# A point of start, a bank and two planning times moved in a Nyström attention and MLP kernel

## The chip, the cores and the metric

The kernel runs on one core of one Trainium2 chip. The metric is device time in microseconds for one execution of the whole program: attention on 8 batches, a two-dimensional Fourier mix, a layer norm and an MLP. The engines are TensorE (PE in the profile, with PEld for its weight loads), VectorE (DVE), ScalarE (ACT), GpSimd (POOL) and SyncE (SP), whose queue issues the DMAs.

## The reference

```python
def _attn_ref(q, k, v):                      # (8, 8, 576, 64) each: batch, head, token, column
    q_lm = q.reshape(B, H, 32, S // 32, D).mean(axis=3)      # 32 landmarks, means of 18 tokens
    k_lm = k.reshape(B, H, 32, S // 32, D).mean(axis=3)
    A, Bm, C = sm(q, k_lm), sm(q_lm, k_lm), sm(q_lm, k)      # scaled softmax of a @ b.T
    Z = Bm.T / (norm(Bm, 1) * norm(Bm, inf) + 1e-06)
    for _ in range(6):
        Z = 2 * Z - Z @ Bm @ Z                               # Newton steps to the inverse
    return A @ Z @ C @ v

def _moe_ref(x, w_ch1, w_ch2):               # x: heads side by side, (8, 576, 512)
    u = x + real(fft(fft(x, axis=1), axis=2))
    un = (u - mean(u)) / sqrt(var(u) + 1e-06)
    return u + maximum(un @ w_ch1, 0.0) @ w_ch2              # 512 -> 2048 -> 512
```

The weights come as 64-bit floats, the rest as 32-bit floats.

## The kernel before

The program is written as a few Python generators ("threads") which take turns while the program is built: `attention` (and the threads it starts), `weights` and `mlp`. Each emits some instructions and then yields a waiting time. `self.now` is the planner's clock: each matmul moves it on by an assumed length, and a thread is taken up again when its time has come, the one of highest priority first. TensorE executes its instructions in just this order. On VectorE, ScalarE and GpSimd a scheduler sets the order; `Timed` (line 114) keeps a planned start for each of their instructions in a log. Where an instruction has a planned arrival `late` (or reads a tile that arrives by DMA), it must stand behind the last instruction of its engine whose planned start is not after `late`. So `late` keeps an instruction from standing ahead of what is planned sooner.

**Weights.** Each of the two matrices comes in NF = 16 pieces. A piece is loaded, decoded from 64-bit to 32-bit floats (`decoded` counts the pieces done, 32 in all), and then halved by `halve` into two fp16 tiles, hi by ScalarE and lo by VectorE (`w<-w,wsc` in the profile; `split_w` counts them). Before w2 can be halved, `scale` finds its scale: `wd`, `wm`, a matmul with ones, `wp_e`, a power on GpSimd (`wp_r`), `wsc`. Once all pieces are decoded, batch 1's q, k and v are loaded.

**MLP.** Tokens go through in chunks `ch` of 256. `h<-unT,w` are the first product's matmuls (24 for one h tile, into one of two h banks, `ps_h`); h is split in two fp16 parts (`u`, `unT`, `h` or `mid` as the room it lies in), and `acc<-w,...` are the second product's (12 for an h tile). The two accumulators of a chunk are read out by `u<-acc,wsc,u`, and only then may the next chunk's second product begin.

**Attention, one batch.** `tokens` sums the landmarks (`lm<-big`: one k sum and two q sums for each of two pairs of head groups, six in all), sums |q| on ScalarE (`amax`), and bounds k and q by powers of two: `kmax`, `qsum`, `aq_e`, `kb`, a matmul `kb,ones`, and `ak_e` (`bound`, line 261). With these it splits k's landmarks (`klm`, `kbd`) and q (`big<-big,aq_r`) into fp16 pairs, and goes on to the scores (`kbd,big`), their softmax (`amx`, `mid`, `asum`) and folds over tokens (`mid<-mid`). `landmarks` takes four of the four banks for attention, `ps_at`, for its matmuls (`at<-lm`, `at<-big,lm`), then makes the landmark softmax (`Bd`, `bs`, `nrm`, `BT`), C's exponentials (`mid<-at,cb`), and the Newton steps (`RE,E`). From batch 2 on, `values` turns C's exponentials over by DMA transposes (`th`) and adds their two parts (`mid<-mid 128x640`). `mix` multiplies everything together (`mid,big`, then `Wx`), with `w<-at,scw,w` and `u<-at,scw,w` on VectorE; `norm` normalises the new tokens (`bn`, `ve`, `r`, `row`). The first four tiles are transposed by TensorE, the later ones by DMA (`unT<-row`).

In batch 1 `tokens` begins when batch 0 is mixed far enough and `split_w[1]` has reached GATE = 8, half of w2. HOLD is an addition to two yields of batch 1 (ahead of the matmul on `kb`, ahead of the landmark matmuls). `there` is the planner's table of when a tile will be ready.

Of the kernel before, what the change touches and what calls it, by code (L numbers as in the profile page):

```python
# [10 lines left out]
F32 = mybir.dt.float32  # L11
# [7 lines left out]
P = 128  # L19
H, S, D, LM, DM, DF = 8, 576, 64, 32, 512, 2048  # L20
NF = DF // P
# [14 lines left out]
MARGIN, NM, AM, M0 = 1.5, 2.0, 2.0, 0.2  # L36

WT = 0.4

GATE = NF // 2  # L40

OFF = 768

PACE = 2

SPARE = 2

HOLD = 2.5

LATER = 5.0  # L50

# [107 lines left out]
class Kernel:  # L159
# [82 lines left out]
    def mm(self, out, a, b, start=True, stop=True, share=1.0):  # L242
        self.there[out.name] = self.now
        self.now += share * (1.0e-3 if a.dtype == F32 else 0.42e-3) * math.prod(b.shape[1:])
        self.nc.tensor.matmul(out, a, b, start=start, stop=stop, skip_group_check=True)  # L245

    def tr(self, out, a, ident):
        self.there[out.name] = self.now
        self.now += 0.11
        self.nc.tensor.transpose(out, a, ident)  # L250
# [7 lines left out]
        self.A.activation(hi, src, AF.Copy, scale=scale)  # L258
        self.V.scalar_tensor_tensor(lo, src, scale, hi, ALU.mult, ALU.subtract)

    def bound(self, cols, n, factor, name):

        ps = self.psum()
        self.mm(ps[:, :n], self.ones16, cols[:, :n])
        return self.power(ps[:, :n], n, factor, name)

# [155 lines left out]
    def tokens(self, b, st):  # L422

        nc, mm, mm3, tr, sm, split = self.nc, self.mm, self.mm3, self.tr, self.sm, self.split
        V, A = self.V, self.A
# [5 lines left out]
        qhs = []  # L431
        for e in range(2):
            kf, qf = loads[e][0][:, 0 : 2 * S], loads[e][1][:, 0:NQ]
            first = V.tensor_reduce(lm[:, 1, e], kf.rearrange("p (m t) -> p m t", t=18), AX.X, ALU.add)
            if b == 1:
                self.tc.keep_in_program_order(first)

            lv = lm[:, 0, e].rearrange("p (x o m) -> p x o m", o=2, m=8)
            qv = qf.rearrange("p (x o t) -> p x o t", o=2, t=2 * SEG)
            for o in range(2):  # L440
                first = V.tensor_reduce(lv[:, :, o], qv[:, :, o, o : o + 144].rearrange("p x (m t) -> p x m t", t=18), AX.X, ALU.add)
                if b == 1:
                    self.tc.keep_in_program_order(first)
            qhs.append(self.big().bitcast(F16))
            A.activation((self.whole[0].bitcast(F16) if b == 0 else qhs[e])[:, 0:NQ], qf, AF.Abs, accum_out=am[:, e : e + 1])
            yield self.till(lm)
        kb = self.small(2, "kb", BF16)
# [5 lines left out]
        V.tensor_tensor(qs, am[:, 0:1], am[:, 1:2], ALU.add)  # L453
        eq, rq = self.power(qs, 1, 2.0**-13, "aq", b == 1)
        V.tensor_tensor(kb[:, 0:1], km, eq, ALU.mult)
        yield self.till(kb, banks=1, more=AM) + (HOLD if b == 1 else 0.0)
        ek, rk = self.bound(kb, 1, 2.0**-13, "ak")
        sc = self.small(2, "sc")
        V.tensor_tensor(sc[:, 0:1], eq, rk, ALU.mult)
        V.tensor_scalar(sc[:, 1:2], ek, 1.0 / 144.0, None, ALU.mult)  # L460
# [19 lines left out]
        for u in range(3):  # L480
            yield self.till(*qhs, banks=1)
            ps = self.psum()
# [27 lines left out]
        for u in range(3):  # L510
            ae, w = aes[u], 512 if u < 2 else 128
            AT = (self.mid() if u < 2 else self.row()).bitcast(F16)[:, 0 : 2 * w].rearrange("p (y t) -> p y t", y=2)
            if b < 2:
                yield self.till(ae, banks=1)
                ps = self.psum()
# [3 lines left out]
            if b >= 2 or u == 2:  # L519
                yield self.till(ae)  # L520
                hl = self.row(2 * w, F16).rearrange("p (y t) -> p y t", y=2)
# [43 lines left out]
    def values(self, b, st, loads, Ces, crs, ci):  # L565

        nc, mm, tr, sm = self.nc, self.mm, self.tr, self.sm
        V, A = self.V, self.A
        R0 = sm.tile([P, 2, 64], F32, name="R0", bufs=1)
        ETs = []  # L570
        for g in range(2):
            yield self.till(Ces[g])
            if b < 2:
                ET = self.mid().rearrange("p (t m) -> p t m", t=5)
                ps = self.psum()
                for t in range(4):
                    tr(ps[:, 128 * t : 128 * t + 128], Ces[g][:, 128 * t : 128 * t + 128], self.ident)
                A.copy(ET[:, 0:4].rearrange("p t m -> p (t m)"), ps)
                ps = self.psum()
                tr(ps[:64, 0:128], Ces[g][:, 512:576], self.ident)  # L580
                A.copy(ET[:64, 4], ps[:64, 0:128])
            else:

                hl, th = (self.mid().bitcast(F16).rearrange("p (y t) -> p y t", y=2) for _ in range(2))
                A.copy(hl[:, 0], Ces[g])
                self.G.tensor_tensor(hl[:, 1], Ces[g], hl[:, 0], ALU.subtract)
                for y in range(2):
                    nc.sync.dma_start_transpose(th[:, y].rearrange("p (t m) -> p t m", m=P), hl[:, y])
                self.there[th.name] = self.there[hl.name] + 4.0
                self.slow.add(th.name)  # L590
                V.tensor_tensor(Ces[g], th[:, 0], th[:, 1], ALU.add)
                ET = Ces[g].rearrange("p (t m) -> p t m", t=5)
            ETs.append(ET)
        for g in range(2):
            yield self.till(ETs[g], loads[0][2], loads[1][2], banks=1)
            vfs = [loads[e][2].rearrange("p (c d) -> p c d", c=5) for e in range(2)]
            ps = self.psum()
            for t in range(5):
                n = P if t < 4 else 64
                for i in range(4):  # L600
                    e, at = divmod(sum(GROUPS, []).index(HEADS[g][i]), 4)
                    v = vfs[e][:n, t, 64 * at : 64 * at + 64]
                    mm(ps[32 * i : 32 * i + 32, 0:64], ETs[g][:n, t, 32 * i : 32 * i + 32], v if at % 2 == i % 2 else v[:, ::-1], t == 0, t == 4)
            V.tensor_scalar(R0[:, g], ps[:, 0:64], crs[g], ci[:, g : g + 1], ALU.mult, ALU.mult)
        st["R0"] = R0

    def landmarks(self, b, st):
# [11 lines left out]
        while b == 1 and self.seconds < NF // 2 - HB:  # L619
            yield 0.5  # L620
        yield self.till(lm, banks=4) + (HOLD if b == 1 else 0.0)
        heads = [(slice(64 * g, 64 * g + 64), slice(32 * r, 32 * r + 32), g, r // 2, r % 2) for r in range(4) for g in range(2)]
# [358 lines left out]

    def attention(self):
        for b in range(self.NB):
            while self.folded < b - 1 or (b > 0 and self.split_w[1] < GATE):
                yield 0.5
            yield from self.tokens(b, {"AT": []})

# [98 lines left out]
```

## Time and profile before

| what | value |
|---|---|
| median of 3 runs | 1006.84 us (1006.77 to 1008.21) |
| the profiled execution | 1008.58 us, of it 1006.8 in the span |
| mean granted TensorE clock | 0.976 |
| TensorE busy | 959.8 us (95%) |
| VectorE, ScalarE, GpSimd busy | 600.5, 333.0, 102.8 us |
| instructions | 20849 |

All times of the trace are microseconds from the first instruction. A profile line gives engine, source line, operation, `out<-in` by tile names, the shape, and a count. Nearly all instructions carry the line of a helper (L138, L245, L250), so they are told apart by their tiles. Lines of waits name the engine, what waited, what it waited for, then the total, the number of times, and the longest.

### The profile page before, as it was taken

The page shows a single profiled execution, that of the slowest core. Times are in us where ns is not written, and L with a number is a line of the kernel's source. Part 1 is how long each engine was busy: PE and PEld are TensorE (multiplying, and loading weights), DVE is VectorE, ACT ScalarE, POOL GpSimd, SP SyncE. Part 2 cuts the span into 40 slices and gives each one's busy share as a digit, 9 for nine tenths or more (in the row PEclk, how much of TensorE's full clock was granted, in tenths as well). Part 3 has the DMA queues.
Part 4 walks back from the last instruction along what each step waited for, and adds up shares of the span by engine and source line. Part 5 has one row for each costly group of instructions (what it writes and reads, how often), then busy time and mean ns, then how long its engine had stood idle before and what let it go on. Part 6 is the DMA issues. An engine that isn't in the chain of part 4 may idle for free.

```text
span 1006.8 us, 20849 instructions
## 1 busy us (share of the span) xinstructions
PE 959.8 (95%) x8698; PEld 666.9 (66%) x8698; DVE 600.5 (60%) x1629; ACT 333.0 (33%) x716; POOL 102.8 (10%) x114
## 2 busy tenths in 40 slices
PE   6869989699999999999999999999999999999998
PEld 4658556467766767667666677676666776666665
DVE  7989876878476836388367736684643935241111
ACT  5668543243224322143224222332322323111110
POOL 0000000003011301032012201120020210010000
PEclk8879989989999999999999999999999999999999
DMA  9854104123302340134211340225020200120000
GB/s 330 290 210 145 62 2 169 22 54 83 136 17 48 63 157 12 32 51 100 100 43 29 45 168 9 55 44 187 1 53 22 53 10 22 22 54 21 1 21 21
DMA packets 97774, 74.66 MB, mean 74 GB/s; under 512 B 68112, under 2 KB 86544, under 8 KB 97552
## 3 DMA queue, kind: packets, MB, share of 16 engines
q1 hardware_dynamic: 97680, 73.34, 25.4%
q8 instruction: 68, 1.11, 0.4%
q14 instruction: 26, 0.21, 0.1%
HBM read 48.02 MB, written 9.44 MB: 57 GB/s over the span
## 4 chain that ended last, share of the span: by engine, by line
PE 86%; DVE 9%; ACT 2%; DMA 2%; issue 1%; POOL 1%; SPq 0%; DVEq 0%; ACTq 0%; POOLq 0%
PE acc L245 36%; PE h L245 36%; PE at L245 13%; DVE w L138 2%; DVE mid L138 1%; DVE u L138 1%; DVE lm L138 1%; DMA big<-k_dram 1%; PE at L250 1%; DVE row L138 0%; ACT w L138 0%; DMA mid<-mid 0%; DMA out_dram<-u 0%; DVE asum L138 0%; DVE bn L138 0%
## 5 line engine op out<-in xcount | busy, mean ns | idle before, releaser
L245 PE MATMUL h<-unT,w 128*128 128x256 f16 x3456 | 411.4, 273 | 6.7 <-DMA unT<-row 5.4
L245 PEld LDWEIGHTS <-w 128*128 128x128 f16 (+1 forms) x3584 | 346.0, 99 | 80.9 <-DMA unT<-row 5.8
L245 PE MATMUL acc<-w,h 128*128 128x512 f16 x1632 | 386.2, 382 | 1.8 <-DVE w L138 1.8
L245 PEld LDWEIGHTS <-h 128*128 128x128 f16 x1632 | 157.8, 99 | 166.6 <-issue 14.2
L138 DVE SCALAR_TENSOR_TENSOR h<-h 128x512 f16<-128x512 f32 x136 | 93.6, 688 | 207.1 <-ACT h L138 206.7
L138 ACT ACTIVATE h<-h 128x512 f16<-128x512 f32 x136 | 81.0, 596 | 319.2 <-PE h L245 313.1
L138 POOL TENSOR_TENSOR r<-ve,mhalf 128x2 f32<-128x2 f32 (+1 forms) x20 | 13.8, 689 | 495.7 <-DVE ve L138 477.0
L138 DVE TENSOR_REDUCE lm<-big 128x32 f32<-128x576 f32 (+1 forms) x48 | 44.4, 938 | 3.3 <-DMA big<-k_dram 3.1
L245 PEld LDWEIGHTS <-big 128*128 128x128 f16 (+1 forms) x864 | 40.5, 104 | 8.5 <-issue 2.1
L138 DVE TENSOR_TENSOR mid<-mid 128x256 f32<-128x256 f32 (+3 forms) x64 | 38.4, 633 | 7.9 <-DMA mid<-mid 6.4
L138 POOL TENSOR_TENSOR mid<-mid 128x640 f16<-128x640 f32 (+1 forms) x24 | 30.6, 1292 | 117.0 <-ACT mid L138 102.5
L245 PEld LDWEIGHTS <-mid 64*128 64x128 f16 (+1 forms) x624 | 29.2, 95 | 17.1 <-issue 10.8
L138 POOL TENSOR_TENSOR row<-row 128x512 f16<-128x512 f32 (+1 forms) x33 | 34.1, 1048 | 50.1 <-ACT row L138 50.1
L138 DVE SCALAR_TENSOR_TENSOR u<-at,scw,w 128x128 f32<-128x128 f32 (+3 forms) x105 | 33.7, 388 | 7.2 <-PE at L245 5.5
L138 ACT CAST row<-row 128x512 f16<-128x512 f32 (+1 forms) x40 | 20.8, 551 | 51.6 <-DVE row L138 44.6
L138 DVE SCALAR_TENSOR_TENSOR w<-at,scw,w 128x262 f32<-128x262 f32 (+1 forms) x42 | 19.1, 486 | 29.7 <-ACT w L138 29.6
L138 DVE SCALAR_TENSOR_TENSOR u<-acc,wsc,u 128x512 f32<-128x512 f32 x36 | 26.9, 749 | 11.8 <-PE acc L245 11.7
L245 PE MATMUL at<-mid,big 128*128 128x262 f16 (+1 forms) x288 | 33.2, 289 | 0.0
L245 PEld LDWEIGHTS at<-RE,E 128*128 128x128 f32 x192 | 26.8, 194 | 8.4 <-issue 2.8
L245 PE MATMUL at<-RE,E 128*128 128x64 f32 (+1 forms) x192 | 28.8, 273 | 3.2 <-DVE E L138 2.5
L138 DVE SCALAR_TENSOR_TENSOR big<-big,aq_r 128x1024 f16<-128x1024 f32 (+1 forms) x32 | 25.8, 840 | 3.5 <-ACT big L138 3.5
L138 DVE TENSOR_TENSOR E<-at,mask 128x256 f32<-128x256 f32 x40 | 16.7, 418 | 18.3 <-PE at L245 18.3
(178 smaller groups left out, 916.8 us busy)
## 6 DMA issues: line engine op xcount, KB each, us to landing
w<-w_dram SPq DMA_DIRECT2D x22, 512.0 KB, 7.0
big<-v_dram SPq DMA_DIRECT2D x16, 640.0 KB, 9.5
big<-q_dram SPq DMA_DIRECT2D x16, 584.0 KB, 6.1
big<-k_dram SPq DMA_DIRECT2D x16, 576.0 KB, 5.2
out_dram<-u SPq DMA_DIRECT2D x36, 256.0 KB, 2.0
big<-w_dram SPq DMA_DIRECT2D x10, 512.0 KB, 6.6
t<-t_dram SPq DMA_DIRECT2D x1, 1048.0 KB, 10.6
unT<-row SPq DMA_TRANSPOSE x64, 2.4
```

The lines of the kernel that those rows point to most:

```text
L138: ins = call(out, *args, **kw)
L245: self.nc.tensor.matmul(out, a, b, start=start, stop=stop, skip_group_check=True)
L250: self.nc.tensor.transpose(out, a, ident)
```

## The change

Batch 1's tokens begin once all 32 pieces are decoded, in place of once half of w2 is halved. HOLD becomes 0. Batch 1's matmul on `kb` writes into an h bank instead of an attention bank. The landmark sums (and `amax` with the first) get `late = now`. The planned arrival of the DMA-transposed C tiles is 6.5 behind the split in place of 4.0.

```diff
-GATE = NF // 2
-HOLD = 2.5
+HOLD = 0.0
-    def bound(self, cols, n, factor, name):
-        ps = self.psum()
+    def bound(self, cols, n, factor, name, apart=False):
+        ps = self.ps_h.tile([P, 512], F32, name="h") if apart else self.psum()
...
             kf, qf = loads[e][0][:, 0 : 2 * S], loads[e][1][:, 0:NQ]
+            V.late = A.late = self.now
             first = V.tensor_reduce(lm[:, 1, e], ...)
...
             for o in range(2):
+                V.late = self.now
                 first = V.tensor_reduce(lv[:, :, o], ...)
...
-        yield self.till(kb, banks=1, more=AM) + (HOLD if b == 1 else 0.0)
-        ek, rk = self.bound(kb, 1, 2.0**-13, "ak")
+        yield self.till(kb, banks=b != 1, more=AM) + (HOLD if b == 1 else 0.0)
+        ek, rk = self.bound(kb, 1, 2.0**-13, "ak", b == 1)
...
-                self.there[th.name] = self.there[hl.name] + 4.0
+                self.there[th.name] = self.there[hl.name] + 6.5
...
-            while self.folded < b - 1 or (b > 0 and self.split_w[1] < GATE):
+            while self.folded < b - 1 or (b > 0 and self.decoded < 2 * NF):
                 yield 0.5
```

No instruction is added or removed; the orders change from w2's scale on. Three places, in the order in which the engines execute (`w_73` is the tensor of w1, `w_74` that of w2; the source lines move by two).

First, VectorE from w2's scale to the landmark sums of batch 1. Before:

```order
L138 TENSOR_SCALAR wp_e<-at 128x1
L138 TENSOR_SCALAR wp_r<-wp_r 128x1
L138 RECIPROCAL wp_e<-wp_r 128x1
L138 TENSOR_SCALAR wsc<-wp_r 128x1
L138 SCALAR_TENSOR_TENSOR u<-h,u 128x512
L138 TENSOR_SCALAR wsc<-wp_e 128x1
L138 SCALAR_TENSOR_TENSOR w_74<-w_74,wsc 128x512 x3
L138 SCALAR_TENSOR_TENSOR unT<-h,unT 128x512
L138 SCALAR_TENSOR_TENSOR w_74<-w_74,wsc 128x512 x5
L138 TENSOR_REDUCE lm<-big 128x64
L138 TENSOR_REDUCE lm<-big 128x4x8 x2
```

After:

```order
L136 TENSOR_REDUCE lm<-big 128x64
L136 TENSOR_REDUCE lm<-big 128x4x8 x2
L136 TENSOR_SCALAR wp_e<-at 128x1
L136 SCALAR_TENSOR_TENSOR u<-h,u 128x512
L136 TENSOR_SCALAR wp_r<-wp_r 128x1
L136 RECIPROCAL wp_e<-wp_r 128x1
L136 TENSOR_SCALAR wsc<-wp_r 128x1
L136 TENSOR_SCALAR wsc<-wp_e 128x1
L136 SCALAR_TENSOR_TENSOR w_74<-w_74,wsc 128x512 x2
L136 SCALAR_TENSOR_TENSOR unT<-h,unT 128x512
L136 SCALAR_TENSOR_TENSOR w_74<-w_74,wsc 128x512
L136 TENSOR_REDUCE lm<-big 128x64
```

The first three sums have moved from behind eight splits of w2 to ahead of its scale, the next three from behind the ninth split to behind the third. On TensorE, the matmul on `kb` stood behind the landmark matmuls, in an attention bank:

```order
L245 MATMUL acc_1680<-w_74,h 128x512
L245 MATMUL at<-lm 32x32 x8
L245 MATMUL at<-big,lm 32x288 x16
L245 LDWEIGHTS ones_102
L245 MATMUL at<-kb,ones_102 128x1
```

and now stands after 18 of the 24 matmuls of an h tile, 27 second-product matmuls ahead of the landmark matmuls:

```order
L243 LDWEIGHTS w_73
L243 MATMUL h<-unT,w_73 128x256
L243 LDWEIGHTS ones_102
L243 MATMUL h<-kb,ones_102 128x1
L243 LDWEIGHTS w_73
```

The bank it writes is one of the two for h.

Second, VectorE where the first chunk's accumulators are read out, in batch 1's softmax. Before:

```order
L138 SCALAR_TENSOR_TENSOR unT<-h,unT 128x512
L138 TENSOR_REDUCE asum<-mid 128x16
L138 TENSOR_TENSOR row<-at,amx 128x128
L138 TENSOR_SCALAR asum<-asum 128x16
L138 SCALAR_TENSOR_TENSOR u<-acc_1680,wsc,u 128x512
L138 RECIPROCAL asum<-asum 128x16
L138 TENSOR_REDUCE asum<-row 128x4
L138 SCALAR_TENSOR_TENSOR u<-acc_1681,wsc,u 128x512
```

After:

```order
L136 SCALAR_TENSOR_TENSOR row<-at,row 128x128
L136 TENSOR_TENSOR row<-row 128x128
L136 TENSOR_TENSOR mid<-mid 128x512
L136 TENSOR_TENSOR mid<-mid 128x256 x2
L136 TENSOR_TENSOR E<-at,mask 128x256
L136 TENSOR_TENSOR mid<-mid 128x256 x2
L136 TENSOR_TENSOR mid<-mid 128x512
L136 TENSOR_TENSOR RE<-RE,at 128x2x32
L136 TENSOR_TENSOR mid<-mid 128x512
L136 SCALAR_TENSOR_TENSOR u<-acc_1683,wsc,u 128x512
L136 SCALAR_TENSOR_TENSOR u<-acc_1684,wsc,u 128x512
```

The two readings now stand behind the folds of batch 1.

Third, VectorE in batch 1's `mix` and `norm`, where batch 2's sums stood. Before:

```order
L138 BN_AGGR mv<-bn 128x2
L138 TENSOR_REDUCE lm<-big 128x4x8
L138 BN_AGGR mv<-bn 128x2
L138 SCALAR_TENSOR_TENSOR h<-h 128x512
L138 TENSOR_SCALAR ve<-mv 128x2
L138 TENSOR_REDUCE lm<-big 128x4x8
L138 TENSOR_TENSOR rt<-r_2574 128x2
L138 TENSOR_REDUCE lm<-big 128x64
L138 SCALAR_TENSOR_TENSOR rt<-rt,ve 128x2
L138 TENSOR_REDUCE kmax<-lm 128x1
L138 SCALAR_TENSOR_TENSOR r_2576<-rt,r_2574 128x2
L138 SCALAR_TENSOR_TENSOR w_74<-at,scw,w_73 128x262
```

After:

```order
L136 BN_AGGR mv<-bn 128x2 x2
L136 TENSOR_SCALAR ve<-mv 128x2
L136 TENSOR_TENSOR rt<-r_2531 128x2
L136 SCALAR_TENSOR_TENSOR rt<-rt,ve 128x2
L136 SCALAR_TENSOR_TENSOR r_2533<-rt,r_2531 128x2
L136 TENSOR_SCALAR row<-u,mv,r_2533 128x512 x2
L136 SCALAR_TENSOR_TENSOR h<-h 128x512
L136 TENSOR_TENSOR row<-row 128x512 x2
L136 SCALAR_TENSOR_TENSOR w_74<-at,scw,w_73 128x262 x2
```

Batch 2's sums have gone behind the second `norm` of batch 1; here `w_73` and `w_74` name rooms at the end of the weights' tensors that `mix` uses. On SP the loads, the stores and the transposes of unT keep their order; in three later batches the last transposes of the softmax tiles are issued in another order among themselves. On GpSimd nothing moves.

## The prediction

> **What bounds the kernel now.** I began with busy time by engine, on the page (share of the span, instructions).
>
> ```profile
> PE 959.8 (95%) x8698; PEld 666.9 (66%) x8698; DVE 600.5 (60%) x1629; ACT 333.0 (33%) x716; POOL 102.8 (10%) x114
> ```
>
> TensorE is busy for 959.8 of 1006.8 us; nothing else comes near. The change removes no matmul and adds none, so it can move the time in two ways only: through the 47 us in which TensorE stands idle, and through the granted clock. The next view is busy time by stretch (PE, PEld, DVE, ACT, POOL, then clock, DMA share, GB/s).
>
> ```profile
> 120.00:140.00 20.00, 14.17 (x98) 5.81 (x97) 17.96 (x58) 10.81 (x24) 0.00 (x0) 0.83 0.00 0
> 200.00:220.00 20.00, 18.82 (x157) 12.40 (x165) 13.51 (x35) 7.74 (x13) 1.42 (x4) 0.82 0.27 55
> 400.00:450.00 50.00, 50.00 (x424) 33.88 (x423) 26.24 (x80) 14.68 (x31) 7.63 (x10) 1.00 0.22 39
> ```
>
> From 120 to 140 TensorE is idle for 5.8 us and its clock at 0.83; from 200 to 220 the clock is 0.82. In the last row TensorE is full, 50.00 of 50.00, as in nearly all later stretches. Up to 109 us the order of the work stays as it is. So the change is decided between 109 and 220 us, in batch 1. Who held TensorE there (waits of PE, 120 to 270 us: total, times, longest):
>
> ```profile
> PE h L245 <- DMA unT<-row: 5.4, 2, 3.2
> PE at L245 <- ACT mid L138: 4.0, 1, 4.0
> PE at L245 <- DVE w L138: 2.4, 1, 2.4
> PE acc L245 <- DVE w L138: 1.8, 1, 1.8
> PE acc L245 <- DVE u L138: 1.4, 1, 1.4
> ```
>
> That is 15.0 us. Two of these waits are followed by slow matmuls; TensorE's timeline (start, length, count, wait ahead):
>
> ```profile
> 112.43 10.90 PE L245 MATMUL acc<-w,mid 128*128 128x512 f16 x48
> 126.04 2.54 PE L245 MATMUL acc<-w,h 128*128 128x512 f16 x11 [1.84 <-DVE w L138]
> 133.75 0.16 PE L245 MATMUL at<-kb,ones 128*128 128x1 bf16 x1 [3.99 <-ACT mid L138]
> 133.78 6.48 PE L245 MATMUL acc<-w,h 128*128 128x512 f16 x18
> 185.31 2.79 PE L245 MATMUL h<-unT,w 128*128 128x256 f16 x24
> 201.18 3.81 PE L245 MATMUL h<-unT,w 128*128 128x256 f16 x17 [2.19 <-DMA unT<-row]
> 204.92 1.52 PE L245 MATMUL at<-mid,big 128*64 128x262 f16 x12
> 307.64 0.86 PE L245 MATMUL at<-mid,big 128*64 128x262 f16 x12
> ```
>
> The fourth row against the second: 18 at the second's pace (11 in 2.54, so 0.215 apart and the last some 0.38 long) are 4.04 us, so 2.4 are lost to the clock. The sixth against the fifth (0.109 apart): 17 are 2.0, 1.8 lost; the seventh against the eighth: 0.7 lost. Waits and clock together are 15.0 + 2.4 + 2.5 = 19.9 us, and the first row is 0.4 over 48 at full pace: 20.3 us could at most be won here.
>
> **Part 1, an earlier start and a bank apart: the wait of 3.99 goes.** The matmul on kb waited for one of four attention banks, all held by the landmark matmuls until ScalarE had read the first. In the h bank, and placed ahead of the landmark matmuls, it waits for kb alone. It costs 0.03 us of TensorE (133.75 to 133.78). No row shows an h bank held for it; the bounds are 0 and one VectorE split of an h tile, 0.68 in the row of 111.13 below. I take 0, because the bank's next h tile comes 24 h matmuls and more later. Gain: 3.99 + 2.4.
>
> **Part 2, what the sums now stand ahead of.** The first three landmark sums stand ahead of the last steps of w2's scale (wp_e), the next three ahead of w2's fourth split, not its ninth and tenth.
>
> ```profile
> 108.89 0.29 DVE L138 TENSOR_REDUCE wm<-wd 128x1 f32<-128x128 f32 x1
> 109.99 0.16 DVE L138 TENSOR_SCALAR wp_e<-at 128x1 f32<-128x1 f32 x1 [0.82 <-PE at L245]
> 110.81 0.15 DVE L138 TENSOR_SCALAR wp_r<-wp_r 128x1 int32<-128x1 int32 x1 [0.66 <-POOL wp_r L138]
> 111.13 0.68 DVE L138 SCALAR_TENSOR_TENSOR u<-h,u 128x512 f16<-128x512 f32 x1
> 112.00 2.47 DVE L138 SCALAR_TENSOR_TENSOR w<-w,wsc 128x512 f16<-128x512 f32 x3
> 119.42 2.67 DVE L138 TENSOR_REDUCE lm<-big 128x64 f32<-128x1152 f32 x3
> 109.87 0.60 ACT L138 ACTIVATE u<-h 128x512 f16<-128x512 f32 x1 [2.53 <-PE h L245]
> 111.25 1.33 ACT L138 ACTIVATE w<-w,wsc 128x512 f16<-128x512 f32 x2 [0.78 <-DVE wsc L138]
> ```
>
> The sums run from 109.1 to 111.8 (2.67); wp_e follows, wp_r 0.82 after it (109.99 to 110.81), the u split inside that gap, and ScalarE's first half of a piece 0.44 after wp_r: 113.0 in place of 111.25. TensorE is there at 112.43, has the first half at 113.7 and VectorE's at 114.5, and loses 0.2 on the next piece: 1.3 + 0.6 + 0.2 = 2.1 us waited. The splits go at 0.86 apart (2.47 for three): two, the unT split, a third to 116.6, three sums to 119.2, the fourth to 119.9. TensorE wants the fourth at 117.95: 1.95. The old wait of 1.84 on the tenth piece and the 0.4 are gone. The sum over |q| (ScalarE) moves into the idle 2.53 ahead of 109.87 and costs nothing; without that cover it would delay the u split by less than those 2.53. No DMA moves here: batch 1's loads are issued at the same place as before, and POOL's order is unchanged.
>
> Then TensorE has 8 matmuls left of the piece (1.7), 24 h (2.6), 27 acc (5.8), the landmark matmuls (1.2) and 18 acc (3.9): it asks for nrm at 135.2. VectorE meanwhile has five splits to 124.4, q's scaling, klm, kbd and five splits more, to 133.1, and only then Bd.
>
> ```profile
> 130.53 0.28 DVE L138 TENSOR_SCALAR Bd<-at 128x32 f32<-128x32 f32 x2
> 133.08 1.26 DVE L138 SCALAR_TENSOR_TENSOR big<-big,aq_r 128x1024 f16<-128x1024 f32 x1
> 134.87 0.18 DVE L138 TENSOR_TENSOR nrm<-diag,rs 128x64 f32<-128x64 f32 x1
> ```
>
> From Bd to nrm were 4.5 us, 1.26 of it q's scaling, which has left; two splits have come in (1.4): nrm at 133.1 + 4.6 = 137.7, a new wait of 2.5. At this point the same matmul work is done as before at 140.1: ahead by 2.4.
>
> **Part 3, the softmax of batch 1.** The score matmuls are now cut into the Newton steps; a bank free only after VectorE's subtraction holds a transpose for 1.0, and one Newton step waits 0.7 behind a split. Then the first accumulator has to be read out (u<-acc) before ch 1's second product may begin. That was placed amid the softmax; now it stands behind all folds.
>
> ```profile
> 153.10 0.75 DVE L138 SCALAR_TENSOR_TENSOR u<-acc,wsc,u 128x512 f32<-128x512 f32 x1
> 153.90 0.81 PE L245 MATMUL acc<-w,u 128*128 128x512 f16 x3 [1.38 <-DVE u L138]
> 158.54 0.28 DVE L138 SCALAR_TENSOR_TENSOR row<-at,row 128x128 f16<-128x128 f32 x1
> 161.98 0.69 DVE L138 TENSOR_TENSOR mid<-mid 128x512 f16<-128x512 f32 x1
> ```
>
> Row split to last fold are 4.1 us (158.54 to 162.67). By the same steps from 137.7 the row split comes at 152.2, so u<-acc runs 156.3 to 157.0; TensorE is ready at 154.0. New wait 3.0 in place of 1.38.
>
> **Part 4, sums behind batch 1's norm.** Four sums of batch 2 stood in the chain from `w` to the transposes.
>
> ```profile
> 184.66 1.34 DVE L138 TENSOR_REDUCE lm<-big 128x64 f32<-128x1152 f32 x1
> 189.01 0.72 DVE L138 TENSOR_REDUCE lm<-big 128x32 f32<-128x576 f32 x1
> 191.42 1.34 DVE L138 TENSOR_REDUCE lm<-big 128x64 f32<-128x1152 f32 x1
> 193.47 0.99 DVE L138 TENSOR_SCALAR row<-u,mv,r 128x512 f32<-128x512 f32 x2
> 194.69 23.71 SPq L907 DMA_TRANSPOSE unT<-row  x10
> ```
>
> Without 1.34 + 0.72 + 1.34 the rows come some 3.3 us sooner against the first mixing matmuls, the transposes too (6.5 us from the first issue to the matmul at 201.18). TensorE now also has 27 acc and 48 h between those matmuls and ch 2's first, 11.0 us at the paces above and some 2 of mixing (12 acc and 24 h before). From the end of the first mixing (185.31) to 201.18 were 15.9 us; less 3.3 that is 12.6, against 13 of work: no wait is left of the 5.4, nor the clock's 2.5. The second `w` now stands behind the row splits, so of the 2.4 wait 0.9 stays.
>
> **Part 5, the rest.** 6.5 for 4.0 in `there` lengthens no transfer, it moves the adds of the transposed tiles in the plan. The one place where such an add held TensorE:
>
> ```profile
> 559.57 0.82 DVE L138 TENSOR_TENSOR mid<-mid 128x640 f32<-128x640 f16 x1 [2.23 <-DMA mid<-mid]
> 560.87 0.63 PE L245 MATMUL at<-RE,E 128*128 128x64 f32 x4 [2.46 <-DVE E L138]
> 561.93 4.45 PE L245 MATMUL acc<-w,h 128*128 128x512 f16 x12
> ```
>
> There the second add stands ahead of E in the new order too: I take 0. It is worth 2.46 + 1.7 (4.45 against 2.75 for 12 at full pace) either way: if it vanished a gain, if batch 2, where one add now stands ahead of ci, repeated it a loss. Batch 2's nrm comes 1.0 late by the same walk (its sums begin later). In batches 3 to 7 TensorE's work ahead covers the later sums (the full row of 400 us); bounds plus or minus 1 us, taken as 0.
>
> **The clock.** 2.46 us idle were enough for the slow matmuls just shown; after 1.84 the row at 126.04 ran at full pace. The new waits are 2.1, 1.95, 2.5 and 3.0; I count one slow stretch, 2.5 us, like the other two. [...]
>
> **Sum.** Gone: 3.99 + 2.4 + 1.84 + 0.4 + 1.38 + 2.4 + 5.4 + 2.5 = 20.3. New: 2.1 + 1.95 + 2.5 + 1.7 + 3.0 + 0.9 + 1.0 + 2.5 = 15.7. Net -4.6: a span of 1002.2 for 1006.8. The profiled run took 1008.58, 1.8 over its span; the median of the runs, 1006.84, stands at the span itself, so I forecast 1002.2.
>
> **Rivals.**
> - The clock stays full: the new waits are spread and each is under 3.2. The same sum without 2.5: 999.7. For it: 1.84 left the clock at full; against it: 2.46 did not, and 2.5 and 3.0 are expected. [...] 0.22.
> - The waits only change place: every wait of 2 us and over brings a slow stretch (three, not one): 1002.2 + 5 = 1007.2, no change; with two 1004.7. 0.18.
> - Slower: ch 2's first matmuls still wait for the transposes. For it: the walk leaves them 0.4 us of slack, and they are one queue (ten within 23.71 us). If something holds them there, the 5.4 and 2.5 stay: 1002.2 + 7.9 = 1010.1. Against it: nothing new stands ahead of them on SP. It decides from some 5 us later than walked (0.4 of slack, 4.2 of wait and the clock's 2.5 take back 6.7, to 1008.9). 0.10.
> - The new waits are mostly hidden, as my walk errs towards waiting (it adds every semaphore step): 995. 0.08.
>
> **How the numbers follow.** The forecast has 0.42, its own range 999.9 to 1004.5. From 996.5 to 1007.5 lie the forecast, the full clock and the changed places, 0.82; 995 and 1010 lie outside. A difference under 0.2% (2 us) is about what a measurement can't tell from none. Faster by more, below 1004.8: 0.41 + 0.22 + 0.08 = 0.71; within, 1004.8 to 1008.9: 0.19; slower: 0.10.
>
> **What would show it.** In the new trace: no wait ahead of kb; PE waits on `w` near 112 and 118 us, on nrm near 135, on `u` near 154; ch 2's first h matmuls without a wait on unT; clock under 1.00 in at most one stretch between 120 and 220. Wrong would be: a wait of over 3 us on unT, or new waits beyond 260 us.

## The result, and the profile after

The changed kernel took 1021.43 us (median of 4 runs, 1020.36 to 1022.83) against 1007.40 for the kernel before: 1.014 times as long (95% interval 1.0122 to 1.0157). The forecast was 1002.2, in a range to 1007.5: it is slower, not faster. The profiled execution took 1020.54, of it 1018.5 in the span. Busy time by engine:

```profile
PE 963.1 (95%) x8698; PEld 667.6 (66%) x8698; DVE 600.4 (59%) x1629; ACT 331.2 (33%) x716; POOL 99.7 (10%) x114
```

TensorE is busy 3.3 us longer for the same matmuls but for the bank of one (963.1 against 959.8). The granted clock does not explain that, for its mean was 0.979 here and 0.976 before; it stays open. The other 8.4 us of the longer span are idle time. Busy time by stretch (TensorE's stands first, its clock third from the end), the three rows shown of before and one more:

```profile
120.00:140.00 20.00, 17.99 (x166) 10.38 (x165) 18.91 (x66) 13.71 (x29) 0.00 (x0) 1.00 0.01 1
200.00:220.00 20.00, 18.17 (x165) 11.72 (x163) 17.53 (x59) 9.12 (x21) 3.06 (x5) 1.00 0.23 58
400.00:450.00 50.00, 50.00 (x419) 33.24 (x417) 25.15 (x59) 13.24 (x23) 6.89 (x9) 1.00 0.22 38
310.00:330.00 20.00, 17.44 (x134) 9.85 (x133) 15.82 (x53) 8.70 (x20) 1.78 (x2) 0.83 0.11 34
```

Batch 1 is better than before: from 120 to 140 us TensorE stands idle for 2.0 in place of 5.8 us, and the clock is full. The row at 400 us, on which the prediction leant for batches 3 to 7, is as full as it was. But from 310 to 330 us there are 2.6 us of idle time and a clock of 0.83. TensorE's timeline in batch 1:

```profile
113.17 0.38 PE L243 MATMUL acc<-w,mid 128*128 128x512 f16 x1 [1.10 <-ACT w L136]
119.33 1.02 PE L243 MATMUL acc<-w,mid 128*128 128x512 f16 x4 [1.75 <-DVE w L136]
136.89 0.46 PE L243 MATMUL at<-nrm,ones_bd 128*128 128x128 f32 x2 [2.01 <-DVE nrm L136]
156.02 5.73 PE L243 MATMUL acc<-w,u 128*128 128x512 f16 x18 [2.70 <-DVE u L136]
201.62 2.78 PE L243 MATMUL h<-unT,w 128*128 128x256 f16 x24
```

These are the waits that the prediction named, at the places it named; ch 2's h matmuls run without a wait on unT. TensorE's waits beyond 200 us, of the changed kernel (the first four rows) and, beyond 210 us, of the kernel before (the last two):

```profile
PE at L243 <- ACT mid L136: 6.2, 4, 2.4
PE at L243 <- DVE E L136: 5.5, 2, 3.0
PE at L243 <- DVE u L136: 5.1, 2, 2.6
PE at L243 <- DVE nrm L136: 0.5, 1, 0.5
...
PE at L245 <- DVE E L138: 2.5, 1, 2.5
PE at L245 <- DVE u L138: 1.6, 2, 0.8
```

17.3 us against 4.1: the loss lies beyond batch 1. Three chains carry it. The first, in batch 2 (timelines of VectorE, ScalarE and TensorE):

```profile
209.99 0.28 DVE L136 TENSOR_REDUCE kmax<-lm 128x1 f32<-128x128 f32 x1
211.01 2.81 ACT L136 ACTIVATE big<-big,aq_r 128x1024 f16<-128x1024 f32 x4 [3.66 <-DVE kb L136]
213.72 0.24 ACT L136 ACTIVATE Bd<-Bd 128x64 f32<-128x64 f32 x1
213.99 0.22 DVE L136 TENSOR_REDUCE bs<-Bd 128x2 f32<-128x64 f32 x1 [1.47 <-ACT Bd L136]
215.45 0.16 PE L243 MATMUL at<-kb,ones 128*128 128x1 bf16 x1 [1.29 <-ACT mid L136]
```

The sums, `kmax` and q's bound come so late that ScalarE, idle for 3.66 us, splits q just when Bd's exponential is due. VectorE waits for it with `bs`, and `cb` behind; so the exponentials that would free an attention bank come late, and TensorE waits for that bank with `kb`. The second, also in batch 2, and the third, in batch 3:

```profile
225.68 0.82 DVE L136 TENSOR_TENSOR mid<-mid 128x640 f32<-128x640 f16 x1 [2.21 <-DMA mid<-mid]
228.04 0.71 PE L243 MATMUL at<-RE,E 128*128 128x64 f32 x4 [3.00 <-DVE E L136]
...
319.98 0.28 DVE L136 TENSOR_SCALAR Bd<-at 128x32 f32<-128x32 f32 x2
320.55 0.98 DVE L136 SCALAR_TENSOR_TENSOR u<-at,scw,w 64x256 f32<-64x256 f32 x3
321.07 1.72 PE L243 MATMUL at<-big,lm 64*32 64x288 f32 x16 [2.56 <-DVE u L136]
322.72 4.02 PE L243 MATMUL h<-unT,w 128*128 128x256 f16 x18
```

An add waits 2.21 us for its DMA ahead of E; and the last `u` of a mix, which frees the bank of the landmark matmuls, now stands behind Bd, and with it behind two of q's splits (1.54 us from 318.53). The 18 h matmuls after that wait take 4.02 us (2.13 at 206.83 in the same trace, where the clock is 1.00): from 320.6 to 327.4 us the granted clock is 0.50.

### The profile page after: what moved, and what is told of

It is laid out like the page before. It is cut to its first block, busy times and chain, and to the rows that moved or that the text cites. A ratio compares the mean times of both kernels' runs of the same rounds, so it can differ in the third digit from the quotient of the medians.

```text
span 1018.5 us, 20860 instructions
## 1 busy us (share of the span) xinstructions
PE 963.1 (95%) x8698; PEld 667.6 (66%) x8698; DVE 600.4 (59%) x1629; ACT 331.2 (33%) x716; POOL 99.7 (10%) x114
## 4 chain that ended last, share of the span: by engine, by line
PE 64%; DVE 8%; issue 4%; ACT 2%; DMA 1%; POOL 1%; SPq 1%; POOLq 0%; DVEq 0%; ACTq 0%
PE h L243 28%; PE acc L243 27%; PE at L243 10%; DVE lm L136 1%; DVE big L136 1%; DVE u L136 1%; DVE h L136 1%; DMA mid<-mid 1%; ACT big L136 1%; DVE mid L136 1%; POOL row L136 1%; DVE row L136 1%; SPq L588 0%; DVE cmx L136 0%; ACT h L136 0%
## 5 line engine op out<-in xcount | busy, mean ns | idle before, releaser
L243 PE MATMUL acc<-w,h 128*128 128x512 f16 x1632 | 382.2, 380 | 0.0
```

## The experiments

In the table each ratio is to the kernel before on the same chip.

| run | us | ratio, 95% interval |
|---|---|---|
| n1_no_late | 1006.54 | 0.9982 (0.9967 to 0.9998) |
| n2_late_alone | 1022.91 | 1.0142 (1.0113 to 1.0171) |
| n3_four_back | 1023.93 | 1.0157 (1.0127 to 1.0187) |
| n4_start_alone | 1004.45 | 0.9959 (0.9945 to 0.9973) |
| n5_bank_for_all | 1026.63 | 1.0186 (1.0165 to 1.0206) |
| n6_late_but_3_and_7 | 1016.32 | 1.0081 (1.0060 to 1.0102) |
| n7_start_and_bank | 1005.77 | 0.9979 (0.9968 to 0.9990) |
| n8_start_adds_behind | 1000.87 | 0.9933 (0.9917 to 0.9950) |
| n9_changed_adds_behind | 1013.36 | 1.0052 (1.0034 to 1.0070) |
| n10_best_plus_bank | 1002.56 | 0.9935 (0.9911 to 0.9960) |
| n11_best_hold_0 | 1000.86 | 0.9917 (0.9892 to 0.9942) |
| n12_best_late_in_2 | 997.78 | 0.9896 (0.9865 to 0.9927) |
| n13_no_late_for_q | 1013.96 | 1.0054 (1.0037 to 1.0071) |
| n14_late_for_q_alone | 1012.66 | 1.0041 (1.0024 to 1.0057) |
| n15_best_late_sums_all | 1008.93 | 1.0004 (0.9991 to 1.0017) |

**Which part of the change.** The first leaves `late` out, the second puts it alone into the kernel before, the third undoes 6.5, the fourth is the start alone.

```diff
-            V.late = A.late = self.now
-                V.late = self.now
```

> The changed kernel without its three assignments of late = now to the landmark sums and the sum over |q|; start, bank, HOLD and 6.5 stay. TensorE's order is the changed kernel's, instruction for instruction; on VectorE the sums of batches 2 to 7 go back to amid the norm and mix of the batch before, as in the kernel before. Theory 1 (the loss lies in the sums' late: kb, Bd, cb and the last u of a mix come late on VectorE, and TensorE waits for them): the waits beyond 200 us fall from 17.4 us to about 4, the slow clock behind them at 229, 317 and 787 us goes with them, and the time is 1000 to 1005. Theory 2 (the loss comes from the earlier start, which shifts the batches against the MLP): 1016 to 1021, waits on kb's bank remain. Theory 3 (the loss comes from the 6.5): 1016 to 1021, the wait of 3.0 on E near 228 us remains.

> The kernel before with the three assignments of late = now alone. TensorE's order is that of the kernel before, instruction for instruction. Theory 1: waits on an attention bank ahead of kb in several of batches 2 to 7, and on u ahead of the landmark matmuls of batches 3 and 7 (about 2.6 us each, each with a slow clock behind it): 13 us of new waits and some 5 of clock, less the 5 us or so that the wait on unT near 200 us gives back: 1015 to 1021. Theories 2 and 3: within 1004 to 1009, since neither the start nor the 6.5 is changed.

```diff
-                self.there[th.name] = self.there[hl.name] + 6.5
+                self.there[th.name] = self.there[hl.name] + 4.0
```

> The changed kernel with 4.0 in place of 6.5; the rest of the change stays. In VectorE's order one add of batch 2's DMA-transposed tiles still stands ahead of ci and E, and both of batch 5's do. Theory 1 and theory 2: 1018 to 1023, the waits on kb's bank, u and E all remain. Theory 3: the time falls to 1012 or below, and the wait of 3.0 on E near 228 us is under 1.

> The kernel before with the start of batch 1 alone (once all pieces are decoded); no late, no bank apart, HOLD 2.5, 4.0. Theory 1: no new waits beyond 220 us of more than 1 us; the gains of batch 1 come in part, as kb still waits for an attention bank: 1001 to 1007. Theory 2: 1014 to 1021, with the waits of the changed kernel beyond 200 us. Theory 3: 1001 to 1007.

TensorE's waits beyond 200 us, without `late` (the first two rows) and with `late` alone (the main three):

```profile
PE at L243 <- DVE E L136: 2.5, 1, 2.5
PE at L243 <- DVE u L136: 1.6, 2, 0.8
...
PE at L245 <- DVE u L138: 5.1, 2, 2.6
PE at L245 <- ACT mid L138: 4.6, 3, 2.1
PE at L245 <- DVE E L138: 2.5, 1, 2.5
```

Without `late` the waits are those of the kernel before; with it alone, in TensorE's old order, most of the new ones are there, and the time is the changed kernel's. Theory 1 holds. Theories 2 and 3 fall: the start alone is faster, and with 4.0 the wait on E in batch 2 stays (2.90 us). Theory 1's times were a little too short: 1006.54, 1022.91 and 1023.93 us lie 0.9 to 1.9 above their ranges. The wait on E in batch 2 is not there with `late` alone, so it needs another part of the change as well, and that is not the 6.5.

Since TensorE's order is the same with and without `late`, the two traces can be laid side by side. The table gives the time from one batch's first Newton matmul to the next one's, and from the last of these to the end of TensorE's last matmul:

| from, to | changed | no late | longer | waits that differ |
|---|---|---|---|---|
| batch 1, 2 | 87.9 | 85.7 | 2.2 | kb 1.29, nrm 0.54, E 3.00; w 0.53 for 2.20 |
| batch 2, 3 | 109.4 | 103.7 | 5.7 | u 2.56 for 0.78 |
| batch 3, 4 | 123.7 | 121.4 | 2.3 | kb 1.65 |
| batch 4, 5 | 106.4 | 105.3 | 1.1 | kb 0.91 |
| batch 5, 6 | 107.7 | 108.4 | -0.7 | kb 2.37 |
| batch 6, 7 | 130.7 | 126.8 | 3.9 | u 2.55 for 0.80 |
| batch 7, end | 208.7 | 208.7 | 0.0 | none |

The sum is 14.5; the waits in the last column make 11.6 of it. Some 1.6 of the rest are the clock, by an estimate: from batch 1's first Newton matmul on TensorE worked for 16.6 us at a clock of 0.5 in the changed kernel and for 13.5 without `late`, and half of such time is counted as lost. It was slow behind batch 2's E and both waits on `u` in the changed kernel (0.50 for 3.4 us from 228.5, 6.8 from 320.6 and 3.4 from 791.7), behind batch 1's `w` and batch 5's E without `late` (0.83 from 190 to 200 us; 0.92 from 550 to 560, 0.74 from 560 to 570); hence the -0.7. The remaining 1.3 are not told apart.

**What each wait is worth.** An h bank for `kb` in all batches; no `late` in batches 3 and 7; the adds written behind their planned arrival.

```diff
-        yield self.till(kb, banks=b != 1, more=AM) + (HOLD if b == 1 else 0.0)
-        ek, rk = self.bound(kb, 1, 2.0**-13, "ak", b == 1)
+        yield self.till(kb, banks=0, more=AM) + (HOLD if b == 1 else 0.0)
+        ek, rk = self.bound(kb, 1, 2.0**-13, "ak", b > 0)
```

> The changed kernel (1021.4 us) with an h bank for the matmul on kb in all batches from 1 on, not batch 1 alone. The orders of all engines are the changed kernel's; only the bank differs. Theory A (the matmul on kb waits for the bank itself, held by a landmark half whose exponential waits for a late cb; nothing behind it needs a bank so soon): the waits of 1.3, 1.65, 0.9 and 2.4 us ahead of kb go, and the time falls by 5 to 8 to 1013 to 1017. Theory B (cb and Bd are late themselves, so the next matmul that needs a bank or nrm waits instead): the same time stands ahead of nrm or of the transposes, 1019 to 1022. Theory C (the bank is now missed by the next h tile, since ak_e, which reads it, stands behind the whole landmark softmax on VectorE): new waits of an h matmul, 1021 to 1030.

```diff
+            if b not in (3, 7):
                 V.late = A.late = self.now
...
+                if b not in (3, 7):
                     V.late = self.now
```

> The changed kernel (1021.4 us) without late in batches 3 and 7 alone; TensorE's order is unchanged, and on VectorE the last u of a mix again stands ahead of Bd in these two. Theory A (those two waits of 2.6 on u, and the slow clock of 8 to 10 us behind each, are the dearest part of the loss): both fall to 0.8 and the slow clock after them goes: 1.8 and some 3.5 of clock each, 10 in all, 1010 to 1013. Theory B (the slow clock has another cause, and comes back elsewhere): only 2 times 1.8 goes, 1017 to 1019.

```diff
-                V.tensor_tensor(Ces[g], th[:, 0], th[:, 1], ALU.add)
+                ths.append(th)
...
+        for g, th in enumerate(ths):
+            yield max(0.0, self.there[th.name] - self.now)
+            V.tensor_tensor(Ces[g], th[:, 0], th[:, 1], ALU.add)
```

> The changed kernel (1021.4 us), with the adds of the DMA-transposed tiles written behind the planned arrival, so that they stand behind E in all batches. Theory A (the waits of 3.0 and 2.5 us on E in batches 2 and 5 come from the adds ahead of it): both waits go, with the slow clock near 230 us: 1012 to 1017; the waits on kb's bank (7 us) and on u (5 us) stay. Theory B (E is late in batch 2 because the late sums push everything behind them): the wait of 3.0 stays at 2 or more, 1017 to 1022.

The bank gained nothing and cost some 5 us (1.0186 against 1.0140). TensorE in batch 2 with the h bank, and two of that run's waits beyond 200 us:

```profile
217.98 0.16 PE L243 MATMUL h<-kb,ones 128*128 128x1 bf16 x1 [1.40 <-DVE h L136]
...
PE at L243 <- DVE nrm L136: 2.2, 2, 1.8
PE at L243 <- DVE RE L136: 2.3, 1, 2.3
```

`kb` now waits for an h tile's split, 1.40 for 1.29, and elsewhere `nrm` (0.5 before, 2.2 now) and RE take over. Theory B has the waits right, but the time lies above its range; theory C has the time in its range, but no h matmul waits in this trace. So the bank was the place where lateness showed, not its cause; why the time grew by 5 us is not told apart. Leaving out batches 3 and 7 brought 5.1 us, between what theory A and theory B expected: each wait on `u` fell to 0.8, and the slow clock behind both (6.8 and 3.4 us long in the changed kernel, not 8 to 10) went: 1.00 from 310 to 340 and from 780 to 810 us. That near 230 us, behind E, stayed (0.83 from 230 to 240); a wait of 1.7 us on RE in batch 6 is new. With the adds behind E both waits on E are gone, and the time falls by 8.1 us; theory A. Of these 5.5 are the two waits, the rest is not told apart.

**Which late.** One of the two engines' assignments is left out in each.

```diff
-            V.late = A.late = self.now
+            V.late = self.now
```

> The changed kernel (1021.4 us) without late on the sum over |q| (ScalarE); late on the landmark sums (VectorE) stays. TensorE's order is the changed kernel's. Theory A (the late sum over |q| holds qsum and aq_r back, ScalarE splits q just ahead of the exponential of Bd, and TensorE waits for kb's bank, nrm and E): the waits on kb's bank (7 us), nrm (0.5) and batch 2's E (3.0) go, those on u in batches 3 and 7 (2.6 each) and batch 5's E stay: 1008 to 1013. Theory B (the landmark sums on VectorE do it): 1018 to 1022.

```diff
-            V.late = A.late = self.now
+            A.late = self.now
...
-                V.late = self.now
```

> The changed kernel with late on the sum over |q| alone, and none on the landmark sums. On VectorE the sums stand amid norm and mix as in the kernel before, but in batches 3 and 7 the last u of a mix still stands behind Bd. Theory A (late on the sum over |q| is enough): waits on kb's bank of 1 us and more in several batches, on u in batches 3 and 7: 1010 to 1017. Theory B (only both together do it, since kmax and qsum are early enough with early sums): 1005 to 1009.

Waits beyond 200 us with `late` on the landmark sums alone (three rows), then on the sum over |q| alone (two):

```profile
PE at L243 <- DVE u L136: 4.5, 2, 2.3
PE at L243 <- ACT mid L136: 3.8, 4, 1.5
PE at L243 <- DVE lm L136: 1.3, 1, 1.3
...
PE at L243 <- DVE u L136: 3.3, 2, 1.7
PE at L243 <- ACT mid L136: 2.0, 2, 1.4
```

Neither alone explains it (1013.96 us lies just above theory A's range for the first, 1012.66 in theory A's for the second): above the run without `late` (0.9982) the sums cost 0.7%, the sum over |q| 0.6%, both together 1.6%. Of these three runs only the one with both, the changed kernel, has the wait of 3.0 on E in batch 2. My theory A for the first was too simple: q is split early there, but the wait on `kb`'s bank in batch 2 stays at 1.30, since Bd now stands behind `kmax` and q's splits on VectorE.

**A version that beats both.** The start alone still has batch 5's wait on E. The runs put the adds behind E, and then the other parts on top.

> The kernel before with the start, the bank of batch 1's kb and HOLD 0: the change without late and without 6.5. With late and 6.5 left in stood 1006.5 for late out alone, and 1004.5 for the start alone. Theory A (the bank and HOLD 0 cost the 2 us: waits on nrm and on u<-acc in place of the one on kbd): 1005.5 to 1008. Theory B (the 6.5 cost them, by other matmuls of the plan in batches 2 to 7): 1003 to 1005.

> The start alone (1004.5 us), and the adds of the DMA-transposed tiles are written in the code after the two transposes' planned arrival, so that on VectorE they stand behind E in every batch, in batch 5 too. Theory A (batch 5's wait on E comes from the two adds ahead of it): the wait of 1.9 on E near 555 us goes, with a slow clock behind it in some runs: 1000.5 to 1003. Theory B (E is late for another reason, or the folds behind the adds are now waited for): 1004 to 1007.

> The start with the adds behind E (1000.9 us), and batch 1's kb matmul in an h bank; HOLD stays 2.5. All orders are the same but for this bank. Theory A (with the earlier start kb waits for no bank any more, so the bank apart does nothing): 1000 to 1002. Theory B (an h bank held until ak_e has read it delays the next h tile, as in the run with the bank for all batches): 1002 to 1004, with a wait of an h matmul near 127 us.

```diff
-HOLD = 2.5
+HOLD = 0.0
```

> The start with the adds behind E (1000.9 us), with HOLD 0: batch 1's landmark matmuls come ahead of its scores, as in the changed kernel. Theory A (HOLD 0 is what cost the 2 us of the bank and HOLD together): the waits of 2.5 on kbd, 1.2 on mid and 1.1 on row go, those of 2.0 on nrm, 0.9 on RE and 2.7 on u<-acc come: 1001.5 to 1004.5. Theory B (the order at this place is indifferent): 1000 to 1001.5.

```diff
+            if b == 2:
+                V.late = self.now
             first = V.tensor_reduce(lm[:, 1, e], ...)
...
+                if b == 2:
+                    V.late = self.now
                 first = V.tensor_reduce(lv[:, :, o], ...)
```

> The start with the adds behind E (1000.9 us), and late = now for the landmark sums of batch 2 alone. TensorE's order is unchanged. Theory A (what late wins ahead of the mix of batch 1 it loses at kb and Bd of batch 2): the wait of 2.2 on w near 186 us falls to 0.5, waits of 1.3 ahead of kb and 0.5 on nrm come: 1000 to 1002. Theory B (without an add ahead of E the late sums of one batch do no harm): 998 to 999.5.

> The start with the adds behind E (1000.9 us), and late on the landmark sums of all batches, none on the sum over |q|. With late in batch 2 alone it was 997.8. Theory A (the late sums are harmless but for the last u of a mix, which stands behind Bd in batches 3 and 7): two waits of 2.6 in place of 0.8, with a slow clock behind each: 1001 to 1006. Theory B (no harm at all): 997 to 999. Theory C (late sums bring back the waits on kb's bank): 1006 or more.

Waits of TensorE from 120 us on, the start with the adds behind E (two rows), the same with `late` in batch 2 (two rows), and with HOLD 0 up to 200 us (two rows):

```profile
PE at L243 <- DVE kbd L136: 2.5, 1, 2.5
PE at L243 <- DVE w L136: 2.2, 1, 2.2
...
PE at L243 <- DVE kbd L136: 2.5, 1, 2.5
PE at L243 <- DVE w L136: 0.5, 1, 0.5
...
PE acc L243 <- DVE u L136: 2.7, 1, 2.7
PE at L243 <- DVE nrm L136: 2.0, 1, 2.0
```

With the adds behind E batch 5's wait on E is gone, and the time is 3.6 us below that of the start alone (1004.45 and 1000.87, on two chips; by the ratios, 0.9959 and 0.9933, it is 2.6, and their intervals just overlap). The bank for batch 1's `kb` changes nothing (0.9935; its 1002.56 us lie in theory B's range, but no h matmul waits near 127 us), HOLD 0 swaps one set of waits for another at the same time (0.9917), so that neither theory of a 2 us cost is borne out; 0.9979 for start, bank and HOLD 0 without the adds against the start's 0.9959 (intervals that overlap) stays open. `late` in batch 2 alone takes the 1.7 us out of the wait on `w` and brings no new one: 997.78 us, 0.9896, the shortest time here. That is theory B by its waits; the interval of the ratio still overlaps that without this `late` (0.9917 to 0.9950), so the gain itself is not clear of noise. In all batches it loses that again and more (1008.93): `u` 4.5, the bank 2.5, `lm` 1.3; theories A and C each had a part of it, A the waits on `u`, C those on the bank.

Why is it free in batch 2 there? ScalarE in that run, q's first split and Bd's exponential:

```profile
202.66 1.16 ACT L136 ACTIVATE big<-big,aq_r 128x1024 f16<-128x1024 f32 x1 [1.39 <-DVE aq_r L136]
213.71 0.26 ACT L136 ACTIVATE Bd<-Bd 128x64 f32<-128x64 f32 x1 [6.63 <-DVE Bd L136]
```

The sum over |q| is not held back, so q is split from 202.66 on, 11 us ahead of Bd, where the changed kernel begins at 211.01. And `kmax` is there (207.32) 3 us ahead of the landmark matmuls (210.32); in the changed kernel it comes 1.1 us behind their start (209.99, 208.89). Both seem to be needed: in the changed kernel without `late` on the sum over |q| the split of q was early too (206.07), `kmax` came 1.1 us behind that start (211.75, 210.65), and the wait on the bank stayed.

## Why the prediction was wrong

- **Part 1, the wait on `kb`.** Gone as forecast (3.99 and the clock's 2.4), but the start did it, not the bank: with the start alone `kb` ran in an attention bank without a wait. That an h bank costs nothing held in batch 1 only.
- **Part 2.** 2.1 and 1.95 on `w` were 1.5 (1.10 and 0.41) and 1.75; 2.5 on nrm was 2.01. Right, and a little high throughout.
- **Part 3.** 1.7 in the softmax was 0.88 (one Newton step; no transpose waited), 3.0 on `u` was 2.70. Right in kind, and the first about twice too high.
- **Part 4.** The waits on unT went, for half of the reason given: without `late`, sums amid the norm, they are gone too, and with `late` alone 3.6 of the 5.4 stay. The work that the start moves ahead covers the transposes. (Four sums stood in the chain, as the prediction says, but its 3.3 us counts three of them; the fourth, at 190.38, took 0.74.) `late` itself is seen in the wait on `w`, 2.2 without it, 0.5 with it (0.9 forecast).
- **Clock.** One slow stretch was counted, and one came in batch 1: 18 matmuls in 5.73 us for 4.04, 1.7 lost for the 2.5 forecast, with the clock at 0.50 from 156.8 to 160.2 us. It came behind 2.70 us of idle TensorE, under the 3.2 of the rival with the full clock; behind 1.75 and 2.01 the clock stayed at 1.00. That it was one stretch is in part luck: the row of 2.46 against that of 1.84 gave the prediction a rule by the length of a wait, and in the last section a wait of 1.64 has a slow clock behind it and one of 2.54 has not.
- **Part 5, the step that failed.** "In batches 3 to 7 TensorE's work ahead covers the later sums (the full row of 400 us); bounds plus or minus 1 us, taken as 0." From batch 2's first Newton matmul on it was 12.3 us against the run without `late` (5.7 + 2.3 + 1.1 - 0.7 + 3.9, with the slow clock behind batch 2's E in the first). The row was true and stayed true, but it lies between the places where the sums are waited for: `kb` at 450, 555 and 664 us, the landmark matmuls at 318 and 788 us. The kernel before shows these last two with a wait of 0.8 each already, so there was no cover there at all. I had walked the six sums of batch 1 one by one, and not one of the later batches, where the same lines act.
- **Batch 2.** 1.0 was given for nrm; nrm took 0.54, but `kb` 1.29 and E 3.00 were not in the sum. E was named as a risk, and the mechanism named, an add ahead of it, is right: with the adds behind E the wait is gone. But it was put down to the 6.5: with 4.0 the add still stands ahead of E and the wait stays, while without `late` the add stands behind E and the wait goes, though the 6.5 stands. The 6.5 itself is worth nothing that the runs can tell (0.9979 without it, 0.9982 with it), as taken.
- **The rivals.** None was this one; the slower rival (a wait on unT) did not come. "New waits beyond 260 us" was named as what would make the prediction wrong, and that is what came.

## What to carry to other kernels

An edit in a loop acts in every pass: walk one later pass at the instruction that waits for the moved work, and read the cover there, not from a full stretch between such places. A delay put on work that several engines hand on is paid twice, here by VectorE's sums and by ScalarE's split of q ahead of an exponential. Where TensorE's order is fixed by a plan, a later place for a side engine's work paid here only where a wait showed that the work in front was late (the `w` of batch 1), so try it in that one pass first.

## What was not expected of the hardware

Two nearly equal waits were followed by different clocks. TensorE's timeline in the run with `late` on the sum over |q| alone, in batch 3 and in batch 7:

```profile
321.70 1.23 PE L243 MATMUL at<-big,lm 64*32 64x288 f32 x16 [1.69 <-DVE u L136]
322.87 2.14 PE L243 MATMUL h<-unT,w 128*128 128x256 f16 x18
...
784.51 1.23 PE L243 MATMUL at<-big,lm 64*32 64x288 f32 x16 [1.64 <-DVE u L136]
785.68 3.70 PE L243 MATMUL h<-unT,w 128*128 128x256 f16 x18
```

After 1.69 us the 18 h matmuls took 2.14 (clock 1.00 from 320 to 330 us), after 1.64 us 3.70 (0.83 from 780 to 790). In the changed kernel 2.56 was followed by slow matmuls, and 2.37 (ahead of `kb` in batch 6) was not. So the length of one idle stretch does not decide it here. The granted clock as the traces of the kernel before and of the changed kernel record it shows more: in both it is 1.00 or 0.50, and it stays at one value for 3.413 us or a whole multiple of it, but for the last value, which ends with the record (between 100 and 960 us it is slow for 6.83, 10.24 and 3.41 us before, for 3.41, 3.41, 6.83 and 3.41 us after). So each of the two traces can be cut into steps of 3.413 us, counted from its first record. Busy time in the steps around the changed kernel's wait of 2.56 on `u` (first two rows) and of 2.54 on E in batch 5 (last three):

```profile
317.20:320.61 3.41, 1.31 (x38) 0.54 (x35) 3.41 (x9) 0.30 (x2) 0.00 (x0) 1.00 0.41 154
320.61:324.03 3.42, 2.96 (x23) 1.34 (x24) 2.94 (x16) 0.26 (x1) 0.00 (x0) 0.50 0.02 5
562.96:566.38 3.42, 2.01 (x54) 1.83 (x52) 1.41 (x5) 0.60 (x1) 0.00 (x0) 1.00 0.73 69
566.38:569.79 3.41, 2.28 (x34) 1.59 (x35) 3.41 (x7) 0.00 (x0) 0.00 (x0) 1.00 0.00 0
569.79:573.20 3.41, 3.41 (x27) 2.42 (x25) 3.41 (x12) 1.52 (x4) 0.00 (x0) 1.00 0.00 0
```

Of the wait on `u` 2.1 us lie in one step, and the next step runs at 0.50. A border cuts the wait on E into 1.4 and 1.1, and the clock stays full. The 2.37 ahead of `kb` was cut too, into 1.0 and 1.3. Counted over the two traces, between 100 and 960 us: a step at full clock with 2.0 us or more of idle TensorE was followed by a slow step in 7 of 7 cases, one with under 1.5 in none of 482, and one between these (1.65 and 1.79 us, both in the changed kernel) in neither case. Where the waits of 1.69 and 1.64 lay in such steps was not shown. In the changed kernel between 100 and 960 us seven waits were 2 to 3 us long: four (2.70, 3.00, 2.56 and 2.55) had 2.1 us or more of idle time in one step and a slow clock behind them; three (2.01, 2.54 and 2.37) had 1.4 at most, and the clock stayed at 1.00. So there such a wait brought a slow clock or not by where it fell on these steps.
